# Infini-attention between linear-attention layers, fp32 on one core: half a query projection ahead of the first row maxima, their transposition three slots later, and one segment's row statistics ten slots later

## Chip, core and metric

One core of a Trainium2 chip. The metric is the time of one execution of the whole program in microseconds (us), as the median of several runs. Beside the runs there is one profiled execution, from which all durations below come. A run's own time contains a little more than the span, which reaches from the first to the last instruction in the trace.

The engines are named as in the profile: PE (TensorE, matmuls), PEld (TensorE's weight loads), DVE (VectorE), ACT (ScalarE), POOL (GpSimd), SP (SyncE, which issues most transfers; SPq and ACTq are the queues of transfers of SP and ACT). DVE, ACT and POOL carry out their own instructions strictly one after the other in the order of the program, and so does PE.

## The reference

Input: x of 2048 tokens and 512 channels, float32. Four layers in the order A, B, A, B, each with a layer norm in front and a residual sum behind.

```
x = A_x                                    # (1, 2048, 512), H = 32 heads of 16
x = x + _A_ref(_layernorm(x), wqkv, w_phi, wo)
x = x + _B_ref(_layernorm(x), wq, wk, wv, wo, beta)
x = x + _A_ref(_layernorm(x), ...)
x = x + _B_ref(_layernorm(x), ...)

# A: linear attention, phi = [softmax(x w_phi), softmax(-x w_phi)]
kv = phi_k^T v;  z = sum(phi_k);  o = (phi_q kv) / (phi_q z + 1e-6);  return o @ wo

# B: infini attention in N = 4 segments of L = 512 tokens
for s in range(4):
    logits = qs @ ks^T * Dh**-0.5 + mask
    a_dot  = softmax(logits) @ vs
    a_mem  = (elu1(qs) @ M) / (elu1(qs) @ z + 1e-6)
    o      = g * a_mem + (1 - g) * a_dot       # g = sigmoid(beta)
    M, z   = M + elu1(ks)^T vs, z + sum(elu1(ks))
return concat(o) @ wo
```

## The kernel before

**Products.** A product of two float32 matrices is made of three matmuls of rounded parts: high times high, high times low, low times high. In the trace they read `g<-w,hh` and `g<-w,hl` for tokens (`hh`, `hl` are the high and low part of the normalised input), and `g<-hh,wqk` and `g<-hl,wqk` for a query or key projection. The results go to PSUM. The bank names are the tiles' tags: `g` is a ring of four banks, `mx` and `my` have one bank each, `lg` is a double bank for logits.

**A layer B** (class `LayerB`) is one loop over slots. Its function `steps` counts a slot number k from -25. From slot 0 on, five slots (R = 5) are one piece: a segment has eight pieces m of four heads, and four segments make 32 pieces. What happens in a slot stands in tables of words. `FIRST`, `GAPS` and two others tell it for the slots from 0 on. The table `BEFORE` tells it for slots -25 to -11, that is in front of the loop. "q1/2" means: two steps, six matmuls, of the query projection of the second channel group (`proj(0, 1, "q")`, 12 matmuls with 512 columns); "k1/2" is the same for keys. In what follows they are q1 and k1. "max0" is `put_maxima(0)`, "v2" a part of a value projection.

**Maxima.** The softmax needs each row's largest logit before its logits are made. `maxima(m)` computes for each piece the logits of all rows on PE (`g<-e,e`, `mx<-e,e`, `my<-e,e`; `e` holds the stacked queries and keys) and takes the maxima on DVE straight out of PSUM, each by an instruction (`g<-g,mask`, `mx<-mx,mask`) and a read-out (`mxs<-`). In front of the loop, from slot -17 to -8, each slot does one fifth of a piece: five for m = 0 (slots -17 to -13), five for m = 1 (-12 to -8). Odd slots use two banks of the ring `g`, even slots the banks `mx` and `my`. `put_maxima(m)` then transposes the 128 x 16 maxima on PE into the bank `mx` (`mx<-ident,mxs`), ACT copies them with changed sign to `mt` (`mt<-mx`), and one slot later ACT's queue sends them into a row of the stacked queries (`e<-mt`). `attend(m)`, from slot 0 on for m = 0, reads that row with its logits (`lg<-e,e`).

**Behind a projection.** When its 12 matmuls are issued, ACT copies the result (`tb<-g`), and in the next slot casts the high part (`ta<-tb`); DVE then makes the low part (`ta<-tb,ta`, a subtraction). SP's queue stacks them into `e` (`e<-ta`).

**What sets the order.** Every instruction of PE, DVE, ACT, POOL and SP is kept in the order in which the Python code issues it (`held` and `Ordered`). Within a slot `steps` first advances `attend` and `maxima`, then does what was put off from the slot before, then feeds work of the layer A ahead (slots -14 to -4: output products `g<-w,oh`, `g<-w,ol`), and last does the words of the table.

**The row statistics.** The second layer A is fed piece by piece into the last segment of the first loop of B (`pass1`). There `upcoming(1)` makes a generator for the layer norm of that layer's second segment: one step loads its rows; four take a row tile's mean and variance each (`moments`: BN_STATS, BN_AGGR on DVE, into the tile `st`); then follow `guard` (DVE), `root` (two ACT instructions), `refine` (six small DVE instructions) and the normalisations on ACT (`x<-x,st`). In the loop of eight `values()` the code takes a step of that generator from the fourth pass on; the list `plan` takes the next ones at the numbered steps j of the key and query stage that follows.

Of the kernel before, what the change touches and what calls it, by code (L numbers as in the profile page):

```python
# [93 lines left out]
7.0 max pt pt fin | 7.1 P/4           | 7.2 P/3           | 7.3 P/3 | 7.4 P/2  # L94
"""
BEFORE = {-25: "load q0", -24: "sq0 sq1", -23: "k0", -22: "sk0 n n", -21: "sk1 v0/2 n n", -20: "v0/2 n n",
          -19: "n n", -18: "v1 n n", -17: "q1/2", -16: "q1/2", -15: "k1/2", -14: "k1/2", -12: "max0", -11: "v2"}


@with_exitstack  # L100
def interleave_kernel(ctx, tc, x_in, a_wqkv, a_wphi, a_wo, b_wq, b_wk, b_wv, b_wo, b_beta,
# [123 lines left out]
    def load_w(key, src=None, tag="w8", low=dve):  # L225
        w = []
        for _ in bring(w, key, src, tag, low):
            pass
        return w
# [176 lines left out]
    def norm_T(xsrc, s, hT, spare=None, slow=False, off=False):  # L406

        st = T2("st", 2, shape=(P, 4, 8))
        xt = rows_of(xsrc, s)
        yield  # L410
        for t, x in enumerate(xt):
            moments(st, t, x)
            if t < 3:
                yield
        guard(st)
        yield
        root(st)
        if slow:
            yield
        refine(st, pool if off else dve)  # L420
        if slow:
            yield
        for t in range(4):
            normal(st, t, xt[t])
            if slow and t < 3:
                yield
        yield
        hT[:] = htiles(spare)
        for t in range(4):
            columns(hT, t, xt[t])  # L430
            yield
# [104 lines left out]
    def v_tile(hT, w, vv, tag, order=range(4), pairs=False):  # L536
        v = sp.tile([P, 4, VROW], F32, tag="v", bufs=2, name=nm("v"))
        vv[:] = [v]
        pool.memset(v[:, :, 0 : H * VW].rearrange("p t (h e) -> p t h e", e=VW)[:, :, :, DH : DH + 1], 1.0)
        pool.memset(v[:, :, H * VW : VROW], 0.0)  # L540
        if not pairs:
            for t in order:
                po = PS(*tag)
                yield from tok_proj(po, hT, t, w)
                act.copy(v[:, t, 0 : H * VW].rearrange("p (h e) -> p h e", e=VW)[:, :, 0:DH],
                         po.rearrange("p (h e) -> p h e", e=DH))
                yield
            return
        for ts in (order[0:2], order[2:4]):
            for n in range(pairs):  # L550
                pos = [PS(*tag) for _ in ts]
                w0, w1 = D * n // pairs, D * (n + 1) // pairs

                def side(po, t):
                    po, lhs, rhs = tok_side(po, hT, t, w)
                    return po[:, 0 : w1 - w0], lhs, lambda b, kc: rhs(b, kc)[:, w0:w1]

                yield from mm3_pair(*[side(po, t) for po, t in zip(pos, ts)])
                for po, t in zip(pos, ts):
                    act.copy(v[:, t, w0 // DH * VW : w1 // DH * VW].rearrange("p (h e) -> p h e", e=VW)[:, :, 0:DH],  # L560
                             po[:, 0 : w1 - w0].rearrange("p (h e) -> p h e", e=DH))
                yield
# [53 lines left out]
    def exp(e):  # L616
        ef = e.rearrange("p h s f -> p (h s f)")
        act.activation(ef, ef, AF.Exp)
# [24 lines left out]
    class LayerA:  # L643
# [65 lines left out]
        def pass1(self, first):  # L709
            hTs, vv = [], []  # L710

            def upcoming(n, off=True):

                h = []
                spare = ("e8" if first else "w8") if n % 2 else None
                return h, norm_T(self.xsrc, SEGS[n], h, spare, slow=True, off=off)

            if first:
                wq, wk, wv, upc = self.first(hTs, vv, upcoming)
            else:  # L720
                norm = norm_T(self.xsrc, SEGS[0], hTs, slow=True, off=True)
                for _ in range(11):
                    next(norm)
                    yield
                wv = load_w("awv")
                for _ in norm:
                    yield
                vt = v_tile(hTs, wv, vv, ("g", G), pairs=1)

                def values():  # L730
                    for _ in range(3):
                        next(vt)

                for _ in range(5):
                    values()
                    yield
                upc = upcoming(1, False)
                next(upc[1])
                for _ in range(3):
                    values()  # L740
                    yield
                for n in range(8):
                    values()
                    if n > 2:
                        next(upc[1])
                    yield
                wk = load_w("awk", None, "e8")
                yield
# [3 lines left out]
            for n, s in enumerate(SEGS):  # L752
# [33 lines left out]
                def kv(t2, n=n, v=v, es=es):  # L786


                    pk = PS(("mx", "my")[t2], 1)[:, 0 : 8 * VW].rearrange("p (g e) -> p g e", e=VW)
                    for g in range(8):  # L790
                        for t in range(2 * t2, 2 * t2 + 2):
                            for j in range(4):
                                h = 4 * g + j
                                mm(pk[32 * j : 32 * j + 32, g, :], lhsT=es[t][:, 32 * h : 32 * h + 32],
                                   rhs=v[:, t, VW * h : VW * h + VW], start=(t == 2 * t2), stop=(t == 2 * t2 + 1),
                                   tile_position=(0, 32 * j))
                    yield
                    if n == 0 and t2 == 0:
                        dve.tensor_copy(kva, pk)
                    else:  # L800
                        dve.tensor_tensor(out=kva, in0=pk, in1=kva, op=ADD)
                    yield

                if n < NSEG - 1:
                    hTs, g = upc
                    vv = []
                    plan = [(j, g) for j in ((0, 2, 3, 4, 4, 8, 9, 11, 13) if n == 0 and not first else (4, 7, 10, 13))]
                    vals, norms = [10 + j * 26 // 16 for j in range(16)], (14, 19, 20, 21, 22, 23, 24, 27, 29, 31, 33)
                    vt = v_tile(hTs, wv, vv, ("g", G))

                    plan += [(j, vt) for j in vals[: 16 if n + 2 < NSEG else 8]]
                    if n + 2 < NSEG:
                        upc = upcoming(n + 2)
                        plan += [(j, upc[1]) for j in norms]
                    plan.sort(key=lambda x: x[0])
                    e = {}

                    def go(late):

                        ready, done = [], []  # L820
                        behind_outs = n == 0 and not first
                        for step in ("k0 k1 q0 q1 k2 k3 v0 q2 q3" if behind_outs else "k0 k1 q0 q1 k2 v0 k3 q2 q3").split():
                            if step == "v0":
                                yield from kv(0)
                                continue
                            t = int(step[1])
                            for j, _ in enumerate((kproj if step[0] == "k" else qproj)(t, e)):
                                if j == 2 and done:
                                    es.append(scale_k(e[done.pop()]))
                                yield  # L830
                            if ready:
                                exp(e[ready[0]])
                                done.append(ready.pop(0))
                            if step[0] == "k" and not (behind_outs and t == 0):
                                ready += [0, 1] if behind_outs and t == 1 else [t]
                            if step == "k1" and late:
                                yield from late

                    for i, _ in enumerate(go(late)):
                        if i == 4 and n == 0 and not first:  # L840
                            wq = load_w("awq", None, "e8")
                        while plan and plan[0][0] <= i:
                            next(plan.pop(0)[1], None)
                        if n == 1 and i % 4 == 0:
                            settle(1)
                        yield
                    for _, step in plan:
                        next(step, None)
                    rest = vt if n + 2 == NSEG else None
                    late = kv(1)  # L850
                    continue
# [704 lines left out]
```

## Time and profile before

| what | value |
|---|---|
| runs | 1367.28, 1372.07, 1366.54 us; median 1367.28 |
| profiled execution, own time | 1365.67 us |
| its span | 1363.9 us |
| mean granted TensorE clock | 0.997 of full speed |
| busy in the span: PE, DVE, ACT, POOL | 97%, 76%, 59%, 51% |
| transfers | 196.27 MB, 144 GB/s in the mean |

A row of the timeline, as the prediction quotes it, reads: start in us from the beginning of the span; duration in us (over all its instructions, where "xN" at the end says that N alike were put together); engine; line of the kernel (that of a helper, so the tiles tell more); operation; output<-inputs with buffer numbers left out; shapes. A bracket at the end gives the engine's idle time just before and what ended it. Successive matmuls overlap in the pipeline, so that the starts of two rows tell more than a duration. The first loop's slots -17 to -8 lie between about 263 and 286 us, the second loop's 665 us later, and the moved statistics between 664 and 672 us.

### The profile page before, as it was taken

What the parts mean: (1) busy time and instruction counts of PE and PEld (TensorE: products, weight loads), DVE (VectorE), ACT (ScalarE), POOL (GpSimd) and SP (SyncE); (2) the same over time, 40 slices, a digit from 0 to 9 for tenths busy, and PEclk for the clock granted to TensorE, in tenths of its full rate; (3) what the DMA queues carried; (4) which work ended last, traced back from release to release, by engine and by line L of the source; (5) the groups of instructions that cost most, each with busy time, mean ns of one, the idle gap of its engine ahead of it and who ended that gap; (6) DMA issues with size and microseconds to landing.
All of it is one profiled execution on the core that took longest, in us unless ns stands there. A gap on an engine that the chain in (4) does not pass through costs nothing.

```text
span 1363.9 us, 36810 instructions
## 1 busy us (share of the span) xinstructions
PE 1316.8 (97%) x14056; PEld 1030.0 (76%) x14056; DVE 1040.8 (76%) x3256; ACT 808.6 (59%) x1201; POOL 696.9 (51%) x1060
## 2 busy tenths in 40 slices
PE   7999989999999999999999998999999999999997
PEld 6888868767777777777668886886777787787764
DVE  4776778778888888888647677787778879878882
ACT  5556345547677677677544433463666866866654
POOL 1568666326447557345324356553356656654442
PEclk9999999999999999999999999999999999999999
DMA  6388447535554545546251103755556554544441
GB/s 204 101 320 276 163 129 231 168 103 141 166 170 133 156 118 134 154 119 180 87 177 41 63 32 125 233 163 139 138 161 171 148 159 101 147 130 100 118 113 45
DMA packets 134400, 196.27 MB, mean 144 GB/s; under 512 B 15440, under 2 KB 61648, under 8 KB 133456
## 3 DMA queue, kind: packets, MB, share of 16 engines
q1 hardware_dynamic: 132256, 193.27, 48.5%
q8 instruction: 112, 1.84, 0.5%
q10 hardware_dynamic: 1968, 0.64, 0.2%
q14 instruction: 64, 0.52, 0.1%
HBM read 101.05 MB, written 39.85 MB: 103 GB/s over the span
## 4 chain that ended last, share of the span: by engine, by line
PE 75%; DVE 11%; ACT 5%; issue 4%; POOL 3%; DMA 2%; SPq 1%; DVEq 0%; ACTq 0%; POOLq 0%
PE g L176 57%; PE lg L176 6%; PE g L180 6%; PE mx L176 3%; ACT P L154 2%; DVE g L154 2%; PE lg L180 2%; POOL P L154 1%; PE my L176 1%; POOL tb L154 1%; DVE my L154 1%; DVE mx L154 1%; DVE mxs L154 1%; DVE es L154 1%; PE mx L180 1%
## 5 line engine op out<-in xcount | busy, mean ns | idle before, releaser
L154 ACT ACTIVATE P<-lg 128x1024 f32<-128x1024 f32 x320 | 329.6, 1030 | 170.9 <-PE lg L176 93.1
L154 POOL TENSOR_SCALAR_AFFINE_SELECT P<-P 128x256 f32<-128x256 f32 (+1 forms) x448 | 193.4, 446 | 293.1 <-ACT P L154 292.6
L154 DVE CUSTOM_DVE_ANT_0 g<-g,mask 128x256 f32<-128x256 f32 (+3 forms) x392 | 191.7, 545 | 9.6 <-PE g L176 9.4
L176 PE MATMUL g<-hh,wqk 64*128 64x512 f32 (+1 forms) x960 | 186.8, 393 | 0.0
L176 PE MATMUL g<-w,oh 64*128 64x512 f32 (+2 forms) x880 | 177.7, 384 | 1.3 <-DVE ol L154 0.7
L154 DVE CUSTOM_DVE_ANT_0 mx<-mx,mask 128x512 f32<-128x512 f32 (+2 forms) x316 | 157.9, 500 | 24.1 <-PE my L176 14.4
L154 DVE CUSTOM_DVE_ANT_0 my<-my,mask 128x512 f32<-128x512 f32 (+2 forms) x316 | 164.2, 519 | 0.0
L176 PE MATMUL lg<-e,e 64*128 64x256 f32 (+2 forms) x1024 | 153.0, 339 | 4.1 <-ACT P L154 4.1
L176 PE MATMUL g<-P,v 128*32 128x128 f32 (+3 forms) x2064 | 151.1, 433 | 4.9 <-DVE mxs L154 4.3
L176 PE MATMUL g<-w,hh 64*128 64x512 f32 (+1 forms) x672 | 143.7, 395 | 2.3 <-ACT w L154 1.3
L154 DVE DVE_READ_ACCUMULATOR2_ANT mxs<- 128x1 f32 x1024 | 145.8, 142 | 0.0
L176 PEld LDWEIGHTS lg<-e,e 64*128 64x128 f32 x1024 | 102.0, 185 | 35.2 <-issue 11.3
L176 PEld LDWEIGHTS g<-P,v 128*32 128x32 f32 x2064 | 61.3, 109 | 88.8 <-issue 62.4
L176 PEld LDWEIGHTS g<-w,oh 64*128 64x128 f32 (+1 forms) x880 | 106.9, 186 | 18.4 <-SPq L154 2.8
L176 PEld LDWEIGHTS g<-hh,wqk 64*128 64x128 f32 (+1 forms) x960 | 105.8, 185 | 16.5 <-PE mx L176 0.7
L154 POOL TENSOR_SCALAR tb<-tb 128x512 f32<-128x512 f32 x72 | 109.1, 1527 | 16.0 <-ACT tb L154 16.0
L176 PE MATMUL g<-w,ol 64*128 64x512 f32 (+2 forms) x440 | 115.6, 377 | 0.5 <-DVE ol L154 0.5
L176 PE MATMUL g<-hl,wqk 64*128 64x512 f32 (+1 forms) x480 | 106.3, 391 | 0.2
L154 ACT COPY tb<-g 128x512 f32<-128x512 f32 (+1 forms) x132 | 71.1, 576 | 48.5 <-PE g L176 46.7
L176 PEld LDWEIGHTS g<-w,hh 64*128 64x128 f32 (+1 forms) x672 | 84.3, 188 | 16.9 <-ACT w L154 1.6
L176 PE MATMUL g<-w,hl 64*128 64x512 f32 (+1 forms) x336 | 90.1, 393 | 0.0
L154 DVE TENSOR_REDUCE es<-P 128x64 f32<-128x1024 f32 x64 | 77.4, 1209 | 12.8 <-ACT P L154 12.8
(149 smaller groups left out, 2888.7 us busy)
## 6 DMA issues: line engine op xcount, KB each, us to landing
e<-ta SPq DMA_DIRECT2D x384, 128.0 KB
wqk<-wqk SPq DMA_DIRECT2D x128, 256.0 KB
x<-x SPq DMA_DIRECT2D x48, 256.0 KB
ot<-in SPq DMA_DIRECT2D x26, 256.0 KB
pq<-tb SPq DMA_DIRECT2D x24, 256.0 KB
tb<-pq SPq DMA_DIRECT2D x24, 256.0 KB
x<-xr SPq DMA_DIRECT2D x22, 256.0 KB
xr<-x SPq DMA_DIRECT2D x20, 256.0 KB
```

Source lines behind the costliest of these rows:

```text
L154: i = f(*a, **k)
L176: return held(nc.tensor.matmul(*a, **k))
L180: return held(nc.tensor.transpose(*a))
```

## The change

Nothing is added or taken away; on each engine the same instructions stand in another order at three places. The whole diff:

```diff
-          -19: "n n", -18: "v1 n n", -17: "q1/2", -16: "q1/2", -15: "k1/2", -14: "k1/2", -12: "max0", -11: "v2"}
+          -19: "n n", -18: "v1 n n q1/2", -17: "q1/2", -16: "k1/2", -15: "k1/2", -11: "v2", -9: "max0"}
...
                 for n in range(8):
                     values()
-                    if n > 2:
-                        next(upc[1])
                     yield
...
-                    plan = [(j, g) for j in ((0, 2, 3, 4, 4, 8, 9, 11, 13) if n == 0 and not first else (4, 7, 10, 13))]
+                    plan = [(j, g) for j in ((0, 0, 1, 1, 2, 2, 3, 3, 4, 4, 8, 9, 11, 13) if n == 0 and not first else (4, 7, 10, 13))]
```

The first edit acts in front of both loops of B. Each half of q1 and k1 moves one slot up, and `max0` from slot -12 to slot -9. The second and third edit move five steps of the generator for the second segment of the second layer A out of the `values()` loop into the stage behind it.

**PE in front of the loop, slots -18 and -17.** Behind the last matmul of a value projection (`g_3425`) stood the first pair of products for maxima (`g_3440`, `g_3441`) and then q1 (`g_3452`):

```order
L176 MATMUL g_3425<-w_2432,hl_3086 128x512
L176 MATMUL g_3440<-e_432_2744,e_431_2743 128x256
L176 MATMUL g_3441<-e_432_2744,e_431_2743 128x256
L176 MATMUL g_3440<-e_432_2744,e_431_2743 128x384
L176 MATMUL g_3441<-e_432_2744,e_431_2743 128x384
L176 MATMUL g_3452<-hh_3085,wqk_2393 128x512
```

Now q1 is `g_3439`, and the maxima's pair is `g_3447` and `g_3448`:

```order
L176 MATMUL g_3439<-hh_3085,wqk_2393 128x512
L176 MATMUL g_3439<-hl_3086,wqk_2393 128x512
L176 MATMUL g_3439<-hh_3085,wqk_2393 128x512 x2
L176 MATMUL g_3439<-hl_3086,wqk_2393 128x512
L176 MATMUL g_3439<-hh_3085,wqk_2393 128x512
L176 MATMUL g_3447<-e_432_2744,e_431_2743 128x256
L176 MATMUL g_3448<-e_432_2744,e_431_2743 128x256
L176 MATMUL g_3447<-e_432_2744,e_431_2743 128x384
L176 MATMUL g_3448<-e_432_2744,e_431_2743 128x384
```

Six matmuls of q1 moved ahead of the pair.

**DVE in front of the loop, slots -16 to -14** (an ISA row with `mask` takes a maximum, one with `mxs` alone reads it out). Before, the low half of q1 (`ta_582`) stood behind the four maxima of slot -15, and the reduction of slot -13 followed the maxima of slot -14 at once:

```order
L154 ISA my_3460,mxs_3439<-my_3460,mask 128x512
L154 ISA mxs_3439 128x1
L154 ISA g_3477,mxs_3439<-g_3477,mask 128x128
L154 ISA mxs_3439 128x1
L154 ISA g_3478,mxs_3439<-g_3478,mask 128x128
L154 ISA mxs_3439 128x1
L154 ISA g_3477,mxs_3439<-g_3477,mask 128x384
L154 ISA mxs_3439 128x1
L154 ISA g_3478,mxs_3439<-g_3478,mask 128x384
L154 ISA mxs_3439 128x1
L154 TENSOR_TENSOR ta_582_3474<-tb_583_3475,ta_581_3473 128x512
L154 ISA mx_3496,mxs_3439<-mx_3496,mask 128x256
```

Now:

```order
L154 ISA my_3472,mxs_3446<-my_3472,mask 128x512
L154 ISA mxs_3446 128x1
L154 TENSOR_TENSOR ta_580_3468<-tb_581_3469,ta_579_3467 128x512
L154 ISA g_3486,mxs_3446<-g_3486,mask 128x128
L154 ISA mxs_3446 128x1
L154 ISA g_3487,mxs_3446<-g_3487,mask 128x128
```

q1's low half (`ta_580`) stands ahead of the four maxima of slot -15. Likewise k1's low half moved from behind the two maxima of slot -13 to ahead of the reduction `es<-P`.

**PE, the transposition.** Before, it stood ahead of the pair of slot -11 (`g_3567`, `g_3568`):

```order
L176 MATMUL g_3512<-w_1993,ol_3272 128x512
L180 MATMUL mx_3563<-ident,mxs_3439 16x128
L176 MATMUL g_3567<-e_432_2744,e_431_2743 128x512
L176 MATMUL g_3568<-e_432_2744,e_431_2743 128x512
L180 MATMUL lg_3576<-ident,P_518_3143 128x128 x4
```

Now it stands directly ahead of the products of slot -8, which write the same bank `mx`:

```order
L176 MATMUL g_3615<-KN_2270,P_548_3282 64x68 x8
L176 MATMUL g_3627<-KN_2270,P_548_3282 64x68 x8
L180 MATMUL mx_3639<-ident,mxs_3446 16x128
L176 MATMUL mx_3643<-e_432_2744,e_431_2743 128x512
L176 MATMUL my_3644<-e_432_2744,e_431_2743 128x512
L180 MATMUL lg_3652<-ident,P_536_3232 128x128 x8
```

On ACT its copy `mt<-mx` and the transfer `e<-mt` moved behind the copies `v<-g` and `P<-lg` in the same way.

**DVE, the statistics** of the second layer A's second segment (`st_9986`). They stood between maxima of the last segment's pieces, and only the refinement stood here, ahead of two additions (`tb_1884`, `tb_1885`). Now (the last two of the four row tiles are shown):

```order
L154 BN_STATS bs_10498<-x_9991 128x6
L154 BN_AGGR st_9986<-bs_10498 128x2
L154 BN_STATS bs_10501<-x_9993 128x6
L154 BN_AGGR st_9986<-bs_10501 128x2
L154 TENSOR_SCALAR st_9986<-st_9986 128x4
L154 TENSOR_TENSOR tb_1880_10268<-g_10432,tb_1880_10268 128x512
L154 TENSOR_TENSOR tb_1881_10269<-g_10433,tb_1881_10269 128x512
L154 TENSOR_TENSOR st_9986<-st_9986 128x4 x2
```

The statistics moved to ahead of the additions and the refinement to behind them. On ACT the two instructions of `root` moved behind several exponentials of logits, to directly ahead of the first two normalisations `x<-x,st`. The orders of SP and POOL are the same as before.

## The prediction

> **What bounds the kernel now.** I read the page first: busy shares and the chain of waits. Then the timeline of each engine in front of both loops and around the moved statistics.
>
> ```profile
> span 1363.9 us, 36810 instructions
> PE 1316.8 (97%) x14056; PEld 1030.0 (76%) x14056; DVE 1040.8 (76%) x3256; ACT 808.6 (59%) x1201; POOL 696.9 (51%) x1060
> PE 75%; DVE 11%; ACT 5%; issue 4%; POOL 3%; DMA 2%; SPq 1%; DVEq 0%; ACTq 0%; POOLq 0%
> ```
>
> PE is busy for 97% of the span. The change adds and removes no instruction, so it can win only PE's idle time, 47 us in all, of which only some lies at the three places that it touches. What PE does and waits for in front of the first loop (a row is start, duration, instruction, and in brackets the idle time before it with what ended it):
>
> ```profile
> 261.64 0.39 PE L176 MATMUL g<-w,hl 128*128 128x512 f32 x1
> 263.02 0.56 PE L176 MATMUL g<-e,e 63*128 63x256 f32 x4 [0.99 <-DMA e<-ta]
> 263.51 0.50 PE L176 MATMUL g<-hh,wqk 128*128 128x512 f32 x1
> 265.09 0.49 PE L176 MATMUL mx<-e,e 63*128 63x512 f32 x1
> 277.46 0.27 PE L180 MATMUL mx<-ident,mxs 128*16 128x128 f32 x1 [2.13 <-DVE mxs L154]
> 277.66 0.50 PE L176 MATMUL g<-e,e 63*128 63x512 f32 x2
> ```
>
> Two waits: 0.99 us of the first maxima for a transfer of stacked rows, and 2.13 us of the transposition for maxima that VectorE is still taking. In front of the second loop the same two stand:
>
> ```profile
> 928.35 0.56 PE L176 MATMUL g<-e,e 63*128 63x256 f32 x4 [1.25 <-DMA e<-ta]
> 942.54 0.27 PE L180 MATMUL mx<-ident,mxs 128*16 128x128 f32 x1 [1.85 <-DVE mxs L154]
> ```
>
> At the moved statistics PE waits 1.28 and 0.21 us for maxima:
>
> ```profile
> 670.13 2.36 PE L176 MATMUL g<-P,v 128*32 128x512 f32 x32 [1.28 <-DVE mxs L154]
> 672.70 0.28 PE L180 MATMUL mx<-ident,mxs 128*16 128x128 f32 x1 [0.21 <-DVE mxs L154]
> ```
>
> These six waits are all that can be won there: 0.99 + 2.13 + 1.25 + 1.85 + 1.28 + 0.21 = 7.71 us.
>
> **Part 1: the projections one slot earlier.** Six matmuls of q1 (1.58 us, from 263.51 to 265.09) now stand in front of the first maxima. PE ran dry at about 261.9, so they cover the 0.99 us, and PE runs 0.99 us ahead from there. The question is what VectorE does with that:
>
> ```profile
> 267.69 0.30 DVE L154 CUSTOM_DVE_ANT_0 g<-g,mask 128x128 f32<-128x128 f32 x1 [0.66 <-PE g L176]
> 270.02 0.69 DVE L154 TENSOR_TENSOR ta<-tb,ta 128x512 fp32r<-128x512 f32 x1 [0.69 <-ACT ta L154]
> 270.63 0.43 DVE L154 CUSTOM_DVE_ANT_0 mx<-mx,mask 128x256 f32<-128x256 f32 x1
> 272.12 1.22 DVE L154 TENSOR_REDUCE es<-P 128x64 f32<-128x1024 f32 x1
> 273.93 0.69 DVE L154 CUSTOM_DVE_ANT_0 g<-g,mask 128x512 f32<-128x512 f32 x1
> 274.54 0.73 DVE L154 CUSTOM_DVE_ANT_0 g<-g,mask 128x512 f32<-128x512 f32 x1
> 275.19 1.09 DVE L154 TENSOR_TENSOR ta<-tb,ta 128x512 fp32r<-128x512 f32 x1
> 276.21 0.29 DVE L154 CUSTOM_DVE_ANT_0 mx<-mx,mask 128x128 f32<-128x128 f32 x1
> ```
>
> The row at 270.02 is the low half of q1's projection. It waits for ScalarE's cast, and today the four maxima of slot -15 (267.69 onward) are done while the cast is awaited. After the change it stands ahead of those maxima. The cast comes no sooner, because ScalarE has four normalisations in front of it, two instructions to a row like the one at 265.45; those wait for POOL's small statistics, which the change does not touch:
>
> ```profile
> 265.45 1.52 ACT L154 ACTIVATE x<-x,st 128x512 f32<-128x512 f32 x2 [1.79 <-POOL st L154]
> 268.77 0.57 ACT L154 COPY tb<-g 128x512 f32<-128x512 f32 x1
> 269.37 0.62 ACT L154 CAST ta<-tb 128x512 fp32r<-128x512 f32 x1
> ```
>
> So VectorE idles from about 267.4 to 270.02 instead of taking 1.49 us of maxima (four of that length last from 270.63 to 272.12). From 270.02 on I add its queue up in the new order: q1's low half 0.61 (to 270.63), maxima of slot -15 1.49 (272.12), of slot -14 1.49 (273.61), k1's low half 0.61 (274.22), the reduction, reciprocal and product that stand between 272.12 and 273.93, 1.81 (276.03), the first maximum of slot -13 0.61 and its read-out 0.14 (276.78). That read-out frees the PSUM bank in which PE's pair of slot -11 is to be written. PE, 0.99 us ahead, meets the waits here instead: about 0.5 us at slot -13's pair, 0.6 at slot -12's, 1.0 at slot -11's, where it starts at about 276.9. That pair lasts 0.43 by the rows at 277.66 (its 0.50 overlaps what follows), so the work behind it begins at 277.3, where before it began at 277.66 + 0.43 = 278.09. PE is about 0.8 us ahead there: 0.99 + 2.13 won, and about 2.1 us plus the moved transposition's own 0.20 to be set against them.
>
> One price of this sum is not certain. k1's low half took 1.02 us (275.19 to 276.21), not 0.61, in its old place, beside POOL:
>
> ```profile
> 274.10 1.06 POOL L154 TENSOR_TENSOR P<-P,rr 128x512 f32<-128x512 f32 x1 [8.68 <-DVE rr L154]
> 275.13 2.95 POOL L154 TENSOR_SCALAR tb<-tb 128x512 f32<-128x512 f32 x2
> ```
>
> In the new order it stands ahead of the reciprocal (rr) for which POOL waits 8.68 us, so POOL is idle then, and I take the 0.61 of q1's twin at 270.02; the bound above is 1.02. The Trainium skill, "SBUF — State Buffer", section "Who interferes with whom", says that a VectorE instruction with two SBUF inputs contends with a GpSimd instruction that reads SBUF, and that the second to issue stands still until the first is through. The row at 275.19, issued 0.06 us behind POOL's, is longer as that says; by the rule the new place gives 0.61, by the row of the old place 1.02, which would make the sum 0.8 us longer over both loops.
>
> SP's order is the same. Its next weights (k1's) are issued as late as today:
>
> ```profile
> 255.17 7.70 SPq L154 DMA_DIRECT2D e<-ta  x12
> 262.97 1.09 SPq L154 DMA_DIRECT2D wqk<-wqk  x2
> ```
>
> k1's first matmuls could start at about 265.9 and may wait for them, at most to their old start at 267.6. That 1.7 us is less than the 2.1 us for which PE waits further on, and VectorE stands still until 270.02 meanwhile: no cost.
>
> **Part 2: the transposition three slots later.** It moves from slot -12's end to right in front of the 128x512 products of slot -8, which write the same bank `mx`. So PE must now wait there for ScalarE's copy out of that bank:
>
> ```profile
> 277.77 0.27 ACT L154 ACTIVATE mt<-mx 16x128 fp32r<-16x128 f32 x1 [4.04 <-PE mx L180]
> 284.03 0.50 PE L176 MATMUL mx<-e,e 63*128 63x512 f32 x1
> 287.75 0.50 PE L176 MATMUL lg<-e,e 64*128 64x512 f32 x2
> ```
>
> From the transposition's start to the copy's end the old place shows 277.77 + 0.27 - 277.46 = 0.58 us, and with a hand-over of about 0.1, 0.65 to 0.7. PE reaches the place 0.8 us before 284.03 and leaves it at about 283.95: **0.1 us won per loop** (0 to 0.2), 0.2 for both. The transfer of the maxima is issued at about 284.1 instead of 278.07; its reader, the first logits at 287.75, stands 3.6 us behind. Nearest for its landing are the transfers in the row at 255.17: the ninth, issued at 255.17 + 8 x 0.64 = 260.3, released PE at 263.02, 2.7 us later. 0.9 us of cover is left.
>
> **Part 3: the statistics.** Their four pairs stood in VectorE's queue between the maxima that PE waits for:
>
> ```profile
> 669.84 0.14 DVE L154 DVE_READ_ACCUMULATOR2_ANT mxs<- 128x1 f32 x1
> 664.84 0.69 DVE L154 BATCH_NORM_STATS2 bs<-x 128x6 f32<-128x512 f32 x1
> 688.37 0.93 DVE L154 TENSOR_TENSOR st<-st 128x4 f32<-128x4 f32 x2
> 690.10 0.17 DVE L154 TENSOR_SCALAR st<-st 128x4 f32<-128x4 f32 x1
> 695.50 1.29 DVE L154 TENSOR_TENSOR tb<-g,tb 128x512 f32<-128x512 f32 x2 [5.22 <-PE g L176]
> 671.38 0.46 ACT L154 ACTIVATE st<-st 128x4 f32<-128x4 f32 x2 [1.88 <-DVE st L154]
> 672.64 0.68 ACT L154 ACTIVATE U<-g,share 128x512 f32<-128x512 f32 x1
> 695.58 1.51 ACT L154 ACTIVATE x<-x,st 128x512 f32<-128x512 f32 x2
> 699.41 0.69 ACT L154 ACTIVATE U<-g,share 128x512 f32<-128x512 f32 x1 [2.32 <-PE g L176]
> ```
>
> Without three such pairs (0.8 us each) in front of them the maxima end over 1.28 us sooner: the wait at 670.13 goes, **1.28 us**. The 0.21 behind it I leave out, because the step after it hangs on U at 672.64, which follows the same product.
>
> In the new place the pairs stand in VectorE's idle time (5.22 us before 695.50). What is late there is the refinement of the square roots: it now follows the two additions, 695.50 + 1.29 = 696.79. It took 690.27 - 688.37 = 1.90 us, with one of its operations slowed to 0.74 (its twins last 0.16); without that 1.33, so it ends at 698.1. Two normalisations (1.51) end at 699.6, and U behind them starts 0.2 us later than 699.41: **0.2 us lost** (0 to 0.8).
>
> **The sum**: 2 x 0.1 + 1.28 - 0.2 = 1.3 us, from 1365.67 of the profiled execution (span 1363.9) to 1364.4. The runs' median lies 1.61 us above the profiled execution, so I forecast 1366.0 us.
>
> **Rivals.**
>
> *All the waits go*, 7.71 us: 1365.67 - 7.71 = 1358.0, as a median 1359.6. For it: PE is 97% busy and gets other work at each place. Against it: VectorE has no instruction less ahead of slot -13, and must stand idle for the cast.
>
> *VectorE's queue is later than I count, and the kernel slower.* The place is the bank of slot -11's pair. If k1's low half costs 1.02 (0.41 more) and the bank is freed only with the second maximum of slot -13 (275.19 - 274.54 = 0.65 more), PE is 1.06 us later than in my sum, a loss of 0.96 in each loop: 1.92 - 1.28 + 0.2 = 0.8 us slower, 1366.5, as a median 1368.1. It decides from 0.65 us of lateness on, where the loops lose what the statistics win. For it: every instruction of that queue is on the path. Against it: the two banks of a pair are freed one by one: the wait at 670.13 ended 0.29 us after the read-out at 669.84, that of the third of four maxima, not of the last.
>
> *The normalisations are late.* With the refinement at its full 1.90 us, U is 0.8 us late: the sum is 0.2 + 1.28 - 0.8 = 0.7, a median of 1366.6. For it: POOL works beside it there. Against it: one of eight such operations was so long.
>
> That the change would not do what it says is excluded by the order of the instructions.
>
> **How the numbers follow.** My forecast 0.50 (its own range 1365 to 1367); all waits gone 0.12; VectorE late 0.15; normalisations late 0.18; something else 0.05. With the median able to shift by some us between sets of runs (1366.54 to 1372.07 here), the range from 1361.0 to 1370.5 leaves out the first rival and the tails, 2 in 10. What a measurement of this kernel can tell from no change is about 0.5%, 6.8 us: below 1360.4 lies most of the first rival, 0.10; above 1374.1 only the unexplained, 0.05; within, 0.85.
>
> **What would show it.** In front of each loop: no wait for a transfer at the first maxima; VectorE idle some 2.6 us ahead of q1's low half; PE waits for maxima at slots -13, -12 and -11 that add up to about 2.1 us; a wait of about 0.4 us for ScalarE's `mt` in front of slot -8's products. At the statistics: no wait in front of the 32 products that stood at 670.13, and U about 0.2 us late at the later place. I am wrong if the three waits in front of the loop add up to under 1 us, or if k1's low half lasts 1 us.

## The result, and the profile after

The changed kernel ran at a median of 1361.84 us (1359.44 to 1364.66, 8 runs), the kernel before beside it at 1366.21 us (1363.65 to 1372.07, 8 runs): a ratio of 0.9967 with a 95% interval of 0.9952 to 0.9983, that is 2.3 to 6.6 us faster. A second set (x9 below) gave 0.9972 (0.9958 to 0.9987).

The page of the kernel after, its span, busy times and chain of waits:

```profile
span 1360.0 us, 36811 instructions
PE 1317.2 (97%) x14056; PEld 1028.9 (76%) x14056; DVE 1040.3 (76%) x3256; ACT 808.7 (59%) x1201; POOL 696.9 (51%) x1060
PE 76%; DVE 11%; ACT 4%; issue 3%; POOL 3%; DMA 1%; SPq 0%; ACTq 0%; DVEq 0%; POOLq 0%
```

The work is the same and PE is busy for as long; the span is 3.9 us shorter. To see where, I took each matmul's start in this trace less the start of the same matmul in the trace of before, and the median of this shift in stretches of unchanged code ahead of and behind each place (by the times of before: 245 to 260 and 288.6 to 296 us for the first loop, 655 to 668 and 676 to 690 for the statistics, 915 to 925 and 953.6 to 962 for the second loop). The difference is what the place won: **0.33 us** in front of loop 1, **1.40** at the statistics, **0.37** in front of loop 2, together 2.1. The rest lies in code that is the same in both: 0.96 us ahead of the first place, and 0.98 between the statistics and loop 2, where the trace of before has a stretch of low clock and this one has none.

PE in front of loop 1 after the change, in the timeline:

```profile
260.68 0.39 PE L176 MATMUL g<-w,hl 128*128 128x512 f32 x1
260.91 0.39 PE L176 MATMUL g<-hh,wqk 128*128 128x512 f32 x1
262.36 0.56 PE L176 MATMUL g<-e,e 63*128 63x256 f32 x4
...
270.01 0.49 PE L176 MATMUL g<-e,e 63*128 63x512 f32 x1
270.96 0.46 PE L176 MATMUL g<-e,e 63*128 63x512 f32 x1 [0.46 <-DVE mxs L154]
272.53 0.38 PE L176 MATMUL mx<-e,e 63*128 63x256 f32 x1 [0.22 <-DVE mxs L154]
274.99 0.49 PE L176 MATMUL g<-e,e 63*128 63x512 f32 x1
275.94 0.50 PE L176 MATMUL g<-e,e 63*128 63x512 f32 x1 [0.45 <-DVE mxs L154]
276.37 0.65 PE L180 MATMUL lg<-ident,P 128*128 128x128 f32 x4
282.34 0.28 PE L180 MATMUL mx<-ident,mxs 128*16 128x128 f32 x1
282.97 0.50 PE L176 MATMUL mx<-e,e 63*128 63x512 f32 x1 [0.35 <-ACT mt L154]
287.20 0.28 PE L180 MATMUL mx<-ident,mxs 128*16 128x128 f32 x1
287.23 0.71 PE L176 MATMUL g<-w,hh 128*128 128x512 f32 x2
```

The times here run 0.96 us ahead of those of before (the first row stood at 261.64). q1 covers the wait for the transfer, and the pair at 262.36 starts without one. In place of the 2.13 us at the old transposition stand three waits for maxima at slots -13, -12 and -11. Their brackets add up to only 1.13 us, but by start times more is lost: the two matmuls of a pair go to different banks and normally start as one (before: one row, 0.43 to the next); here the second of slot -13 starts 0.95 behind the first, and so does that of slot -11. The first matmul's row covers part of the wait. At 276.37 + 0.96 = 277.33 PE is 0.76 us ahead of before (278.09), and after the wait for `mt` at 282.97 only 0.10 us (283.93 against 284.03).

DVE there, with one row from the start of the loop (286.13, used further down):

```profile
269.09 0.69 DVE L154 TENSOR_TENSOR ta<-tb,ta 128x512 fp32r<-128x512 f32 x1 [2.71 <-ACT ta L154]
272.71 0.69 DVE L154 TENSOR_TENSOR ta<-tb,ta 128x512 fp32r<-128x512 f32 x1
273.32 1.21 DVE L154 TENSOR_REDUCE es<-P 128x64 f32<-128x1024 f32 x1
275.74 0.14 DVE L154 DVE_READ_ACCUMULATOR2_ANT mxs<- 128x1 f32 x1
286.13 0.42 DVE L154 TENSOR_TENSOR tmp<-g,r 128x256 f32<-128x256 f32 x1
```

DVE stands still for 2.71 us ahead of q1's low half, with the four maxima of slot -15 queued behind it. k1's low half goes by in 0.61 us (272.71 to 273.32). The row at 275.74 reads out the first maximum of slot -13; the second matmul of slot -11's pair starts 0.20 us behind it.

The statistics, PE first, then DVE and ACT at the later place:

```profile
667.62 2.36 PE L176 MATMUL g<-P,v 128*32 128x512 f32 x32
669.91 0.28 PE L180 MATMUL mx<-ident,mxs 128*16 128x128 f32 x1
670.79 0.66 PE L180 MATMUL g<-ident,U 128*128 128x128 f32 x4 [0.60 <-ACT U L154]
694.40 2.36 PE L176 MATMUL g<-P,v 128*32 128x512 f32 x32
```

```profile
694.12 0.36 DVE L154 TENSOR_TENSOR st<-st 128x4 f32<-128x4 f32 x2
695.12 0.17 DVE L154 TENSOR_SCALAR st<-st 128x4 f32<-128x4 f32 x1
```

```profile
695.33 1.52 ACT L154 ACTIVATE x<-x,st 128x512 f32<-128x512 f32 x2 [1.88 <-DVE st L154]
696.83 0.69 ACT L154 ACTIVATE U<-g,share 128x512 f32<-128x512 f32 x1
```

The 32 products no longer wait, and what follows them waits for U. At the later place the refinement lasts 1.17 us (694.12 to 695.29) and nothing is late: U starts at 696.83, 2.43 us behind the start of its product, as it did before (699.41, with the product at 696.98).

### The profile page after: what moved, and what is told of

Read it like the earlier page. It is cut to its first block, busy times and chain, and to the rows that moved or that the text cites. A ratio compares the mean times of both kernels' runs of the same rounds, so it can differ in the third digit from the quotient of the medians.

```text
span 1360.0 us, 36811 instructions
## 1 busy us (share of the span) xinstructions
PE 1317.2 (97%) x14056; PEld 1028.9 (76%) x14056; DVE 1040.3 (76%) x3256; ACT 808.7 (59%) x1201; POOL 696.9 (51%) x1060
## 4 chain that ended last, share of the span: by engine, by line
PE 76%; DVE 11%; ACT 4%; issue 3%; POOL 3%; DMA 1%; SPq 0%; ACTq 0%; DVEq 0%; POOLq 0%
PE g L176 58%; PE lg L176 6%; PE g L180 6%; PE mx L176 3%; ACT P L154 2%; POOL P L154 2%; DVE g L154 2%; PE lg L180 2%; PE my L176 1%; DVE es L154 1%; POOL tb L154 1%; DVE my L154 1%; DVE mx L154 1%; DVE mxs L154 1%; PE mx L180 1%
```

## The experiments

Eleven kernels ran, each timed beside the kernel before on the same chip. "Won" is the shift worked out as above, from one trace each against the trace of before; plus means lost. "Clock" is the mean over a kernel's runs of (1 - granted clock) x span: an estimate, in us, of the time that a lower clock took. The kernel before, over the 79 runs beside x1 to x11, has 5.5 there; set by set it has 5.7 (beside x1 to x4), 5.2 (x5 to x8), 6.2 (x9 and x10) and 4.3 (x11).

| kernel | median, us | before beside it | ratio (95%) | loop 1 | statistics | loop 2 | clock |
|---|---|---|---|---|---|---|---|
| the change | 1361.84 | 1366.21 | 0.9967 (0.9952 to 0.9983) | -0.33 | -1.40 | -0.37 | 3.2 |
| x9, the change again | 1362.20 | 1365.28 | 0.9972 (0.9958 to 0.9987) | -0.76 | -1.43 | -0.76 | 4.5 |
| x1, before again | 1365.79 | 1365.49 | 1.0002 (0.9989 to 1.0015) | -0.06 | -0.04 | +1.51 | 5.7 |
| x2, loops alone | 1363.59 | 1365.49 | 0.9984 (0.9972 to 0.9996) | -0.38 | -0.38 | -0.73 | 4.5 |
| x3, statistics alone | 1362.51 | 1365.49 | 0.9985 (0.9972 to 0.9998) | -0.07 | -1.44 | +1.59 | 3.8 |
| x4, transposition alone | 1360.68 | 1365.49 | 0.9965 (0.9950 to 0.9981) | -1.76 | -0.16 | -1.94 | 3.7 |
| x5, transposition and statistics | 1360.76 | 1365.66 | 0.9955 (0.9939 to 0.9972) | -1.90 | -1.41 | -1.90 | 5.2 |
| x6, the change, both splits later | 1359.79 | 1365.66 | 0.9953 (0.9938 to 0.9968) | -2.49 | -1.38 | -2.50 | 4.3 |
| x7, projections alone | 1369.64 | 1365.66 | 1.0026 (1.0014 to 1.0037) | +1.17 | -0.02 | +1.21 | 6.6 |
| x8, the change, q1's split later | 1360.10 | 1365.66 | 0.9957 (0.9941 to 0.9973) | -1.90 | -1.41 | -1.90 | 3.8 |
| x10, as x6, transposition in a bank of g | 1358.29 | 1365.28 | 0.9937 (0.9915 to 0.9960) | -1.85 | -1.42 | -2.68 | 3.6 |
| x11, as x10, k1 in its old slots | 1358.13 | 1364.35 | 0.9950 (0.9932 to 0.9967) | -2.73 | -1.40 | -2.71 | 4.4 |

Where a place is unchanged, the shifts stay within 0.4 us, save for +1.51 and +1.59 in loop 2 of x1 and x3, which are stretches of low clock (below).

**x1, the kernel before once more**, with no edit.

> The kernel before once more, against itself. What is asked: how much of the measured 4.4 us is a difference between executions and not of the change. Theory 1 (the trace of the change shows only some 2 us at its three places; the other 2 us are spread between executions): the median lies within 2 us of the kernel before on either side, and this profile differs from the first one in the first 250 us or in a stretch of lower clock by about 1 us, in code that is the same. Rival (the whole 4.4 us belong to the change): medians equal within 0.5 us and the profile follows the first within 0.3 us everywhere.

Theory 1 holds: the medians agree to 0.3 us, and yet the trace is 2.2 us ahead of the first one by 250 us, in the same code, and loses 1.51 us in front of loop 2. A single trace's span is no measure of a change of 2 us; a shift at a place is.

**x2, the loops alone.**

```diff
-          -19: "n n", -18: "v1 n n", -17: "q1/2", -16: "q1/2", -15: "k1/2", -14: "k1/2", -12: "max0", -11: "v2"}
+          -19: "n n", -18: "v1 n n q1/2", -17: "q1/2", -16: "k1/2", -15: "k1/2", -11: "v2", -9: "max0"}
```

> Only the table in front of the loops is changed; the statistics stay. Theory 1, from the drift of the two traces: 0.3 us won in front of each loop, 0.6 to 0.7 in all. Rival (what the trace of the whole change does not show at its places belongs to the loops): 3 us won.

The places show 0.38 and 0.73, the runs 2.2 us with an interval from 0.5 to 3.8. The rival's 3 us is inside the interval, so the runs alone don't exclude it; the trace does not show it.

**x3, the statistics alone.**

```diff
                     values()
-                    if n > 2:
-                        next(upc[1])
...
-                    plan = [(j, g) for j in ((0, 2, 3, 4, 4, 8, 9, 11, 13) if n == 0 and not first else (4, 7, 10, 13))]
+                    plan = [(j, g) for j in ((0, 0, 1, 1, 2, 2, 3, 3, 4, 4, 8, 9, 11, 13) if n == 0 and not first else (4, 7, 10, 13))]
```

> Only the statistics are moved; the table stays. Theory 1: 1.2 us won, the wait of 1.28 us in front of the 32 products at 670 gone and nothing lost at the later place. Rival (what is not shown belongs to the statistics): 4 us won.

1.44 us at the place, 2.0 (0.3 to 3.8) in the runs. 4 us are excluded.

**x4, the transposition alone.** With the two parts of the loop's edit taken apart:

```diff
-          ... -15: "k1/2", -14: "k1/2", -12: "max0", -11: "v2"}
+          ... -15: "k1/2", -14: "k1/2", -11: "v2", -9: "max0"}
```

> Only the transposition moves from slot -12 to -9; the projections and the statistics stay as before, and so does the order on DVE. Theory 2 (the early projection takes back in front of each loop what the late transposition wins, because DVE then stands still for q1's cast): without the early projection DVE's queue stays where it was, PE's 2.13 and 1.85 us of waiting are gone, some 0.4 us come back as a wait for mt in front of slot -8's products, and the 0.99 and 1.25 us for the transfer remain: 1.4 to 1.7 us won per loop, 2.8 to 3.4 in all, which is more than with the whole table. Rival (the late transposition is worth what both edits together show, since DVE's maxima are late anyway and the next bank waits for them): 0.3 us per loop, 0.6 in all.

This is what settles the case. Alone, the transposition wins 1.76 and 1.94 us in front of the loops, two to five times what the whole edit of the table wins there in its three traces (the change, x2, x9), and by its median it is as fast as the whole change though it leaves the statistics where they were. PE's first maxima wait as before, and the only new wait is the one for `mt`:

```profile
262.29 0.56 PE L176 MATMUL g<-e,e 63*128 63x256 f32 x4 [1.24 <-DMA e<-ta]
281.54 0.50 PE L176 MATMUL mx<-e,e 63*128 63x512 f32 x1 [0.36 <-ACT mt L154]
```

**x7, the projections alone.**

```diff
-          ... -18: "v1 n n", -17: "q1/2", -16: "q1/2", -15: "k1/2", -14: "k1/2", -12: "max0", ...
+          ... -18: "v1 n n q1/2", -17: "q1/2", -16: "k1/2", -15: "k1/2", -12: "max0", ...
```

> Only the projections one slot earlier; transposition and statistics as before. Theory 2: the wait for the transfer (0.99 and 1.25 us) is gone, but DVE ends the maxima of slot -12 1.1 us later than before, and the transposition waits for them: 1.1 us lost per loop, the kernel 2.2 us slower. Rival (the early projection is worth the wait that it covers): 2.2 us faster.

The kernel is slower by 0.26% (0.14 to 0.37), 1.17 and 1.21 us at the places. The wait for the transfer is gone, but PE's wait at the transposition grows from 2.13 to 2.63 us, behind new waits at slots -13 and -12:

```profile
269.78 0.46 PE L176 MATMUL g<-e,e 63*128 63x512 f32 x1 [0.43 <-DVE mxs L154]
271.35 0.38 PE L176 MATMUL mx<-e,e 63*128 63x256 f32 x1 [0.22 <-DVE mxs L154]
276.51 0.27 PE L180 MATMUL mx<-ident,mxs 128*16 128x128 f32 x1 [2.63 <-DVE mxs L154]
```

because DVE stands still ahead of q1's low half, and so comes 1.2 us later to the maxima in the bank `mx` that the transposition is to overwrite (their read-out starts at 276.21, in times that run 2.15 us ahead of before, against 277.18):

```profile
267.90 0.69 DVE L154 TENSOR_TENSOR ta<-tb,ta 128x512 fp32r<-128x512 f32 x1 [2.72 <-ACT ta L154]
```

**x6 and x8, q1 early on PE, but its split back behind the maxima on DVE.** x6 puts the split of both projections one slot later, x8 that of q1 alone (its first line ends in `== (0, 1, 0)`, with m).

```diff
+            later = (s, c) == (0, 1)
             for n, f in enumerate(self.projected(s, c, m, pp)):
-                self.at.setdefault(self.k + 1 + n, []).append(f)
+                self.at.setdefault(self.k + 1 + n + later, []).append(f)
```

> The whole change, but the split of q1 and k1 into high and low part one slot later than it, which is the slot of before: DVE takes its maxima again in the order of before, while PE has q1 early. Theory 2: DVE no longer stands still for 2.7 us ahead of q1's low half, the three waits at slots -13, -12 and -11 shrink from 1.13 us together to some 0.5 us at slot -11, and each loop wins 2.1 us against the kernel before: 2 x 2.1 + 1.2 = 5.4 us in all. Rival (DVE's order does not matter, PE is late for another reason): as the whole change, 1.9 us by the traces.

> As the one before last, but with the split of q1 alone one slot later; that of k1 stays early, ahead of the reduction. Theory 2: q1's low half costs nothing more, k1's 0.61 us still stand in front of the maximum of slot -13 that frees the bank for slot -11: 1.5 us won per loop, 2 x 1.5 + 1.2 = 4.2 us under the kernel before, by a little less than with both. Rival (k1's place is the one that counts): as the whole change.

In x8's expectation "the one before last" is x6. Both come out as theory 2 has them, x6 with 2.5 us per loop even above it, x8 with 1.9 instead of 1.5. PE has no wait left at slots -13 to -11 in x6, only the one for `mt` and 0.30 us for k1's weights:

```profile
264.28 0.47 PE L176 MATMUL g<-hh,wqk 128*128 128x512 f32 x1 [0.30 <-DMA wqk<-wqk]
279.86 0.50 PE L176 MATMUL mx<-e,e 63*128 63x512 f32 x1 [0.35 <-ACT mt L154]
```

and DVE no longer idles ahead of q1's low half (268.13), while k1's, back in its old place beside POOL, lasts 1.09 us again without anybody waiting for it:

```profile
268.13 0.69 DVE L154 TENSOR_TENSOR ta<-tb,ta 128x512 fp32r<-128x512 f32 x1
273.30 1.09 DVE L154 TENSOR_TENSOR ta<-tb,ta 128x512 fp32r<-128x512 f32 x1
```

So it is the place of the split in DVE's order, and not the early projection on PE, that took the gain back.

**x5, the late transposition with the late statistics**, projections as before: the edits of x3 and x4 together.

> The late transposition and the late statistics, the projections where they were before. Theory 2: the parts add up, 2 x 1.65 (measured in the trace of x4) + 1.2 = 4.5 us under the kernel before and 2.6 us under the whole change by the traces (which showed some 1.9). Rival (no part costs anything, the early projection is neutral): the same time as the whole change.

The parts add up at the places: 1.90 + 1.41 + 1.90 = 5.2 us. The medians of x5 and of the change lie only 1.1 us apart, with overlapping intervals; the runs of x5 happened to lose more to the clock (5.2 against 3.2).

**x9, the change once more.**

> The whole change once more, with more runs beside the kernel before. Its trace shows 2.1 us at its three places (0.33 and 0.37 in front of the loops, 1.40 at the statistics); the first 8 runs showed 4.4. Theory 1 (the rest lies between executions): the median of these runs is 1.5 to 3.5 us under the kernel before, and the trace shows again 2.1 us at the three places and differences of about 1 us elsewhere. Rival (the whole 4.4 belong to it): 4 to 5 us again.

3.1 us by the medians, 1.8 to 5.7 by the interval. The statistics repeat to 0.03 us, but in front of the loops this trace wins 0.76 twice where the first had 0.33 and 0.37. The reason is one small DVE instruction, shown in the last section.

**x10 and x11, what is left in front of the loop.** x10 sends the transposition of the first piece into the ring g, in slot -10; x11 also moves k1's halves back to slots -15 and -14, with only q1's split late.

```diff
-            pt = PS("mx", 1)
+            pt = PS("g", G) if m == 0 else PS("mx", 1)
...
-          ... -11: "v2", -9: "max0"}
+          ... -11: "v2", -10: "max0"}
```

> The kernel with both parts later, but the transposition of the first piece goes into a bank of the ring g, in slot -10, instead of the bank mx in slot -9. Theory 2 (what is left in front of the loop is the wait for ACT's copy out of mx): the 0.35 us wait in front of slot -8's products goes, 2.85 us won per loop instead of 2.5, so 2 x 2.85 + 1.4 = 7.1 us under the kernel before by the places of the trace. Rival (the ring is too short for one more tile): a new wait for a bank of g in slots -9 to -8 of 0.4 us or more, and no gain over the version before.

> The version before, with k1's two halves back in the slots of the kernel before (-15 and -14) while q1 stays one slot earlier. In the version before, PE's only waits in front of the loops were 1.09 and 0.39 us for k1's weights, and with nothing left to absorb them they stood on the path (1.85 and 2.68 us won per loop, with about 3 expected without them). Theory 2: k1's first matmul starts some 0.5 us later behind the pair of slot -15, so 0.5 and 0.4 us of those waits go: about 2.4 and 3.0 us won, 0.8 us more in all than the version before. Rival (the weights' arrival is not on the path; the difference of the two loops is of another kind): the same as the version before within 0.2 us in either loop.

In x10 the wait for `mt` is gone and no bank of g is waited for. Loop 2 wins 2.68 instead of 2.50, less than the 2.85 expected, and loop 1 wins less than x6: 1.85. PE's only wait there has become k1's weights, 1.09 us late in loop 1 and 0.39 in loop 2:

```profile
266.80 0.47 PE L176 MATMUL g<-hh,wqk 128*128 128x512 f32 x1 [1.09 <-DMA wqk<-wqk]
```

x11 removes that wait, and both loops win 2.7 us, where 2.4 and 3.0 were expected: 0.88 us more than in x10 in front of loop 1, but only 0.03 in front of loop 2. The next wait stands behind it at the same matmuls: a bank that ACT has yet to copy out, behind its normalisations.

```profile
267.20 0.50 PE L176 MATMUL g<-hh,wqk 128*128 128x512 f32 x1 [0.85 <-ACT v L154]
```

x11 wins 6.8 us at its places, more than any other, and x10 5.9; by the runs the two can't be told apart (1358.13 and 1358.29 us). Both beat the kernel before. Every run of x10 is shorter than every run of x9, the change timed beside the same runs of the kernel before; that x11 beats the change rests on its places, since the intervals of the two ratios overlap.

## Why the prediction came out as it did

The forecast was 1366.0 us in a range of 1361.0 to 1370.5, 1.3 us faster; measured were 1361.84, and 3.1 to 4.4 us faster. The direction was right, but the size was only three to four tenths of what was measured. The median lies inside the range, 0.8 us above its lower edge, and outside the 1365 to 1367 that I had given to my own mechanism; that the wide range held is partly luck. Of the 4.2 us between forecast and median, 1.1 come from the kernel before, whose three runs ahead of the prediction had a median of 1367.28 and whose eight had 1366.21.

- **The wait for the transfer goes.** Right: no wait at 262.36.
- **DVE idles some 2.6 us ahead of q1's low half.** Right: 2.71 us here, 2.33 in x9.
- **Three new waits of 2.1 us for maxima, PE about 0.8 us ahead behind them.** Right in the place where PE comes out: 0.76 us ahead, with slot -11's second matmul released by the first maximum of slot -13, as counted. The sign of being wrong that I gave, waits under 1 us together, was badly chosen: the brackets add up to 1.13 us in front of loop 1, but to 0.90 in front of loop 2 and to 0.66 and 0.65 in x9, so the sign came up although the mechanism was right. The first matmul of each pair hides part of the wait, and in x9 DVE idles 0.4 us less.
- **k1's low half at 0.61.** Right: 0.61 us where POOL waits for `rr`, and a row of 1.09 again in x6, where it stands behind POOL's start. The Trainium skill, "SBUF — State Buffer", section "Who interferes with whom", says that the two contend, and on that the runs agree. They do not show that the second stands still until the first is through: before, DVE's row ended at 276.28, while the first of POOL's two instructions from 275.13, of some 1.5 us each, lasted until 276.6.
- **k1's weights cost nothing.** Right for this change: PE waited 0.33 us for them in front of loop 2 and no less was won there, and x2 waited 1.14 us in front of loop 1 and still won 0.38, since PE waits for DVE further on anyway. In x10, with that wait gone, they do cost.
- **A wait of 0.4 us for `mt`, 0.1 us won per loop.** The wait was 0.35 and PE 0.10 us ahead at slot -8's products, as worked out. But 0.33 and 0.37 were won, since I stopped the sum there. In the trace of before PE meets DVE once more at the start of the loop. PE and then DVE there, before:

```profile
288.18 0.28 PE L180 MATMUL mx<-ident,mxs 128*16 128x128 f32 x1
288.50 0.70 PE L176 MATMUL g<-w,hh 128*128 128x512 f32 x2
```

```profile
287.93 0.42 DVE L154 TENSOR_TENSOR tmp<-g,r 128x256 f32<-128x256 f32 x1
```

  `g<-w,hh` started 0.32 us behind the transposition, 0.15 us after DVE's reading of a bank of g had ended (288.35). After the change the same DVE row is 0.84 us earlier by the same times (286.13 + 0.96 against 287.93), and the matmul starts 0.03 us behind the transposition (287.23 and 287.20). That it waited for this bank is read from these times; the profile names no wait there. This term of 0.2 us per loop was missing.
- **The statistics: 1.28 us won, 0.2 lost.** 1.40 to 1.44 won; the refinement took 1.17 us and not 1.33, and nothing was lost.
- **What was mis-sized.** The sum at the places was 1.3 us; the traces show 2.1 and 2.95. Of the 0.8 us up to 2.1, 0.5 were won at the start of the two loops, 0.1 at the statistics, and 0.2 are the loss that did not come; x9's further 0.8 go with the shorter idle time of DVE. The rest of what the runs show goes with the clock, a term which the sum did not have: over 20 runs of the change a lower granted clock took an estimated (8 x 3.2 + 12 x 4.5) / 20 = 4.0 us, over 79 of the kernel before 5.5. The mean times (1362.2 and 1366.0) differ by 3.8; without the clock's share 2.3 are left, which lies between the two traces. Whether the change itself lowers the clock's share is not shown (last section).

Of the rivals, the one with all waits gone is nearest by its number (1359.6), but not by its mechanism: 2.1 to 2.95 of its 7.71 us were won at the places. The late normalisations did not come. My rival of a slower kernel, with DVE's queue later than counted, did not come either: k1's low half took 0.61 us, and the bank came free with the first maximum. A slower kernel does come from the projections alone (x7), by the idle time of DVE that I had counted. In the whole change the late transposition outweighed it: plus 2.4 and minus 3.7 us over both loops, each measured alone, which I had put into one sum without pricing them apart. The sum was small, as measured, and did not show that one half of the edit should have been left out.

## What to carry to other kernels

Where an edit moves two things at one place, cost each alone: here one half alone won 3.7 us at its places and the other alone lost 2.4. Work moved earlier on the bound engine also moves its follow-up earlier in the queues of the others; if that follow-up waits for a third engine (q1's low half for ACT's cast), everything behind it in an in-order queue waits too, so move the producer and leave the consumer where it was. And read a small change by the shift of the same instructions at its place: the span of a single trace can hide it (x3's is 1.0 us longer than that of before, although its place won 1.44).

## What the hardware showed that was not expected

**A clock that drops for 3.4 us, by chance, and mostly behind PE's longer waits.** The rows are stretches of 10 us: busy time of each engine with its count, then the granted clock, the DMA share and GB/s. Before, after, and the kernel before a second time (x1) in front of loop 2:

```profile
840.00:850.00 10.00, 8.14 (x81) 6.65 (x81) 7.90 (x16) 4.06 (x5) 4.53 (x6) 0.83 0.36 123
```

```profile
840.00:850.00 10.00, 7.63 (x96) 6.15 (x95) 8.22 (x19) 5.09 (x6) 6.03 (x6) 1.00 0.08 23
```

```profile
940.00:950.00 10.00, 9.85 (x81) 7.32 (x83) 6.08 (x26) 2.03 (x4) 2.04 (x2) 0.83 0.44 106
```

0.17 x 10 us are 1.7 us of clock, which is 3.4 us at half speed; stretches of 1 us from 840 to 843 show a granted clock of 0.50. In the first stretch twelve matmuls took 4.61 us, in the second the same twelve 3.06:

```profile
839.08 0.46 PE L176 MATMUL my<-v,P 128*32 128x17 f32 x33 [2.23 <-issue]
839.47 4.61 PE L176 MATMUL g<-e,w 128*128 128x512 f32 x12
```

```profile
836.50 0.45 PE L176 MATMUL my<-v,P 128*32 128x17 f32 x33 [2.23 <-issue]
836.88 3.06 PE L176 MATMUL g<-e,w 128*128 128x512 f32 x12
```

Both stand behind the same wait of 2.23 us, so such a wait makes the drop possible, not certain. Of the thirteen traces ten have it there. In front of loop 2, three of the four traces that keep the transposition's place (x1, x3, x7; not that of before) have it, and none of the nine that moved it away, whose longest PE wait there is 1.08 us. In x1 and x3 it stands behind waits of 2.10 and 2.02 us and costs 1.5 and 1.6. In x7 it begins at 937.1, ahead of the transposition's wait and behind waits of 0.49 and 0.20 only, so a long wait is not needed; and it costs nothing there, since PE would have waited anyway (1.43 us instead of the 2.63 of loop 1, and 1.21 lost against 1.17). In front of loop 1 none has it, though PE waits 1.69 to 2.63 us there in the four traces. Drops also stand elsewhere, among others near 20 us in all thirteen, and from about 180 us on in x2, x9 and x11, there over 6.8 us.

The Trainium skill, "TensorE: Matmul & The Clock Gate", part 1, describes a half-rate state decided in free-running windows of about 3.4 us: the length agrees, and so does that the same code is hit in one execution and spared in another. Its section "Why this matters for your kernels" asks for no PE-idle gaps over about 3 us; here that is not enough, since drops followed waits of 2.0 to 2.2 us.

That the clock explains what the runs gained beyond the places is an inference from the means: kernels that keep the wait in front of the loops lost 5.7, 3.8 and 6.6 us (x1, x3, x7) beside 5.5 of before, those without it 3.2 to 5.2. x3 does not fit, and neither do x5 and x11, which lost as much as the kernel before beside them (5.2 and 5.2, 4.4 and 4.3). No kernel was built that fills the wait and changes nothing else, so the cause stays open.

**A DVE instruction of 0.17 us that lasts 1.0 or 1.37.** The statistics' `guard` ahead of the loop's normalisations, 128 x 4 elements, is issued 0.3 us behind an addition of POOL. In the trace of the change and in x9, DVE and then POOL:

```profile
260.88 1.37 DVE L154 TENSOR_SCALAR st<-st 128x4 f32<-128x4 f32 x1
```

```profile
260.56 1.29 POOL L154 TENSOR_TENSOR tb<-tb,tb 128x512 f32<-128x512 f32 x1
261.79 0.43 POOL L154 MEMSET v<- 128x128 f32 x2
```

```profile
263.62 1.00 DVE L154 TENSOR_SCALAR st<-st 128x4 f32<-128x4 f32 x1
```

```profile
263.31 1.29 POOL L154 TENSOR_TENSOR tb<-tb,tb 128x512 f32<-128x512 f32 x1
264.53 0.46 POOL L154 MEMSET v<- 128x128 f32 x2
```

In x9 it ends with the addition (264.62 and 264.60), in the first trace only with the two memsets behind it (262.25 and 262.22); in the trace of before, too, it lasts 1.33 us (from 261.83) and ends with the memsets. ACT's normalisations and the cast of q1 hang on it, so DVE stands still 2.33 or 2.71 us, and a loop wins 0.76 or 0.33: x2 has one of each, 1.37 with 0.38 and 1.01 with 0.73. Which of the two happens differed between executions of the same program; why was not tried.
